# Stores moved to another engine's queue, and sums merged over two hidden units, in the last first layer of a fused attention and feed-forward kernel

## The chip, the cores and the metric

The kernel runs on one core of a Trainium2 chip, in one launch. The metric is device time in microseconds. The engines are TensorE (PE in the profile, its weight loads PEld), VectorE (DVE), ScalarE (ACT), GpSimd (POOL) and SyncE (SP). Any of SP, ACT and POOL can issue a transfer.

## The reference

All data are fp32. An attention block is followed by a feed-forward block on its output:

```python
# q, k, v: (4, 8, 768, 64); centroids: (8, 16, 64)
mask = argmax(q_n @ c_n) [:, None] == argmax(k_n @ c_n) [None, :]
attn = softmax(where(mask, q @ k.T / 8, -1e9)) @ v
x = attn.transpose(0, 2, 1, 3).reshape(4, 768, 512)
xn = (x - mean) / sqrt(var + 1e-6) * g_ln
out = x + maximum(xn @ w_ch1, 0) @ w_ch2      # 512 -> 2048 -> 512
```

## The kernel before, in words

The attention takes the first 318 us of the profiled execution. Then the feed-forward block runs batch by batch, b = 0 to 3. Each batch has a *first layer* (xn @ w_ch1, with the relu) and a *second layer* (with w_ch2, and x added). The first layers are computed at 318 to 390, 466 to 534, 605 to 668 and 737 to 805 us, each followed by its second layer; the program ends at 877.7.

**Fewer products.** Both layers replace a 2x2 block product by seven block products and sums (Strassen's scheme in Winograd's form). In a first layer, `first_layer(b, j, part)` issues one of the parts 1, 2, 6, 5, 7, 4, 3 for unit j; a unit is 128 hidden features of each half of w_ch1's columns, and there are NFH = 8. Each part is four matmuls of 128x384 (L853) into a PSUM bank. `kept` (L877, ACT copies at L879) copies a bank to SBUF, into a tile with the tag "p" (five buffers), when a later part needs it: u2 after part 6, u3 after part 7. `hidden_tile` gives the place of a finished hidden block in SBUF, `add_relu` and `relu` (L890, ACT at L892) complete it. TensorE does the products, DVE the sums.

**Two levels deep.** Second layers of b = 1 to 3 are `deep_layer`: seven ways, each itself seven products of 128x192 (L1149). They need sums of hidden blocks; `outer_sums(c, two)` (L1099) makes them for one unit c with three DVE adds (L1102, L1103, L1105). The finished outputs have features on partitions. `turn` (L1206) turns them by 32x32 transposes on DVE (L1208) into a tile y with the tag "row", of which there are two, and appends eight stores to a list `leaving`, 48 KB each, in runs of 128 B. `leave(n, queues)` issues the first n stores of the list (L1222). It is called from deep_layer and from `unit_end(b, j)`, which runs once for each unit of the next first layer. For b = 1, unit_end calls it also for x_d<-col, 96 KB each, a scratch copy of x for the batches to come.

**The last first layer.** `last_layer(b)`, b = LAST = 3, uses the deeper scheme for three of the seven parts as well. It walks over NPU = 4 pairs of units, g = 0 to 3, with eight slots each. A slot issues one plain part for one unit of the pair, (0,1), (1,1), (0,6), (1,6), (0,7), (1,7), (0,4), (1,4), and after it a few of the inner products A, B and C (`inner_products`, TensorE L1272, sums on DVE at L1281 and L1287, copies on ACT at L1283). B yields `fifth_sum`, the part that both outputs of a unit need. `onto_first` (L1407 to L1412) adds it to u2 and u3 with one DVE add of 128x384 (L1410) per unit and half, in slots 4 and 5 (l = 0) and 6 and 7 (l = 1). Then comes relu for the tiles in `summed`, and outer_sums for the two units of the pair before, one in slot 3 and the other in slot 4.

The orders of PE, DVE, ACT and SP are those of emission, written out by hand. `ring_load` and `last_load` stream weights on SP from scratch in device memory (w<-w_d, and ws<-w_d at L1360). SP also issues all stores of `leave` except in the last deep layer, where they alternate between SP and ACT. POOL issues two stores of y_end (L1504) at the end of the program.

Of the kernel before, what the change touches and what calls it, by code (L numbers as in the profile page):

```python
# [8 lines left out]
F32 = mybir.dt.float32  # L9
# [4 lines left out]
ALU = mybir.AluOpType  # L14
# [9 lines left out]
def kernel(  # L24
# [845 lines left out]
    def hidden_tile(r, f):  # L870

        l, c = divmod(f, NFH)
        h = place((r, l))[:, c]
        hidden[r, l, c] = h
        return h

    def kept(bank, name):  # L877
        t = hid.tile([P, HC], F32, tag="p", name=name, bufs=5)
        nc.scalar.copy(t, bank[:, :HC])  # L879
        return t  # L880

# [13 lines left out]
    def first_layer(b, j, part):  # L895

        _, t1, t2, t4 = normed[b]
        st = sets[b, j]
        s1, s2, s3, s4 = st["s"]
        if part == 1:  # L900
            st["x"] = ps("x_ps")
            product(st["x"], w1_block(0, 0, j), x_block(b, 0, 0), True)
            st["p1"] = kept(st["x"], "p1")
        elif part == 2:
            y = ps("y_ps")
            product(y, w1_block(0, 1, j), x_block(b, 1, 0), True)
            add_relu(0, j, y, st["p1"])
        elif part == 6:
            product(st["x"], s2, t2, False)
            st["u2"] = kept(st["x"], "u2")  # L910
        elif part == 5:
            st["z"] = ps("z_ps")
            product(st["z"], s1, t1, True)
        elif part == 7:
            product(st["x"], s3, x_block(b, 0, 1), False)
            st["u3"] = kept(st["x"], "u3")
            if "z" in st:
                add_relu(1, NFH + j, st["z"], st["u3"])
        elif part == 4:
            product(st["x"], w1_block(1, 1, j), t4, False)  # L920
            nc.scalar.activation(hidden_tile(0, NFH + j), st["x"][:, :HC], AF.Relu)
        elif part == 3:
            product(st["z"], s4, x_block(b, 1, 1), False)
            add_relu(1, j, st["z"], st["u2"])
# [171 lines left out]
        h = h.rearrange("p c (t a r) -> p c t a r", a=2, r=Q)  # L1096
        return [[h[:, l * NQH : (l + 1) * NQH, :, r] for l in range(2)] for r in range(2)]

    def outer_sums(c, two):  # L1099

        a11, a12, a21, a22 = [place((r, l))[:, c] for r in range(2) for l in range(2)]
        nc.vector.tensor_tensor(place("e")[:, c], a21, a22, ALU.add)  # L1102
        nc.vector.tensor_tensor(a21, a11, a21, ALU.subtract)  # L1103
        if two:
            nc.vector.tensor_tensor(place("s")[:, c], place("e")[:, c], a11, ALU.subtract)  # L1105

    def outer_late(o, x, y, n):
# [118 lines left out]


    PAIRED = 2
    LAST = B - 1
    NPU = NFH // 2  # L1230
    w1_d = {n: spill.tile([NPU, P, m], F32, name=f"w1_d{n}") for n, m in ((2, 512), (5, 896), (3, 896), (0, 1024))}
    pairs_of = {}
# [129 lines left out]
    def last_layer(b):  # L1362

        deep_room(b)
        tmp, (_, t1, _, _) = deep[b]["tmp"], normed[b]
        fifth_sum = tmp[:, 2]
        x5 = inner_x(t1, tmp[:, 0])
        x_of = {5: x5}
        t = flat(unit("pi"))
        second = [t[:, i * QC : (i + 1) * QC] for i in range(3)]  # L1370
        third = [last_w["a3"][:, 2 * QC + i * QC : 3 * QC + i * QC] for i in range(2)] + [t[:, 3 * QC :]]
        state = {}

        def first_of(g):

            w = last_w[5]
            return {
                "w": w_operands(*parts_of(w, 3), w[:, 3 * P :]), "x": x_of[5], "onto": None,
                "keep": lambda way: hid.tile([P, HC], F32, tag="p", name="kept", bufs=5)[:, :QC],
                "to": lambda r, h: fifth_sum[:, r * HC + h * QC : r * HC + (h + 1) * QC],  # L1380
            }

        def third_of(g):
            def to(r, h):
                return hidden_tile(1, 2 * g + r)[:, half[h]]

            return {
                "w": w_operands(*parts_of(last_w["a3"], 3), last_w[3]), "x": x_of[3], "onto": to, "to": to,
                "keep": keep_in(third),
            }  # L1390

        def second_of(g):
            (a11, a12), (_, a22) = w1_pair(2 * g)
            return second_pair(b, 2 * g, w_operands(a11, a12, a22, last_w[2]), x_of[2], second)

        makers = {"A": second_of, "B": first_of, "C": third_of}

        def steps(what, g, i):
            if g >= NPU:
                return  # L1400
            if i == 1:
                state[what, g] = makers[what](g)
            inner_products(state[what, g], {1: (1, 2), 2: (6, 5), 3: (7,), 4: (4, 3)}[i])
            if i == 4 and what != "B":
                summed.extend(hidden_tile(int(what == "C"), 2 * g + r) for r in range(2))

        def onto_first(j, l):  # L1407
            h = hidden_tile(1, l * NFH + j)
            first = fifth_sum[:, (j % 2) * HC : (j % 2 + 1) * HC]
            nc.vector.tensor_tensor(h, first, sets[b, j][("u2", "u3")[l]], ALU.add)  # L1410
            if l:
                summed.append(h)  # L1412

        for g in range(NPU):
            j = 2 * g
            for slot, (r, part) in enumerate(
                ((0, 1), (1, 1), (0, 6), (1, 6), (0, 7), (1, 7), (0, 4), (1, 4)), 1
            ):
                if (g, slot) != (0, 1):
                    first_layer(b, j + r, part)  # L1420
                inner = {
                    1: [("C", g - 1, 4), ("B", g, 3)], 2: [("B", g, 4), ("A", g, 1)], 3: [("A", g, 2)],
                    4: [("A", g, 3)], 5: [("A", g, 4)], 6: [("C", g, 1)],
                    7: [("C", g, 2), ("B", g + 1, 1)], 8: [("C", g, 3), ("B", g + 1, 2)],
                }
                if g == 0:
                    inner |= {
                        1: [], 2: [("B", g, 1)], 3: [("B", g, 2), ("A", g, 1)], 4: [("A", g, 2), ("B", g, 3)],
                        5: [("B", g, 4), ("A", g, 3)], 6: [("A", g, 4), ("C", g, 1)],
                    }  # L1430
                elif g == NPU - 1:
                    inner |= {5: [("A", g, 4), ("C", g, 1)], 6: [("C", g, 2)], 7: [("C", g, 3)], 8: [("C", g, 4)]}
                for what in inner[slot]:
                    steps(*what)
                if g == 0:
                    if slot == 2:
                        x_of[2] = inner_x(x_block(b, 1, 0), flat(unit("xi")))
                    if slot == 3:
                        x_sum(b, 3)
                    if slot == 4:  # L1440
                        x_of[3] = inner_x(x_block(b, 1, 1), tmp[:, 1])
                        x_sum(b, 4)
                for r in {4: (0,), 5: (1,)}.get(slot, ()) if g else (0, 1) * (slot == 5):
                    onto_first(j + r, 0)
                if slot in (6, 7):
                    onto_first(j + slot - 6, 1)
                relu(len(summed))
                if slot in (3, 4) and g:
                    outer_sums(j - 5 + slot, True)
                for n, at, ahead in ((0, 7, 1), (5, 3 if g else 5, 1), (3, 2, 0), (2, 6, 1)):  # L1450
                    if slot == at and (ahead or g):
                        last_load(n, g + ahead)
                if slot in (4, 8):
                    unit_end(b, j + slot // 8)
                if slot in (6, 8) and g == NPU - 1:
                    inner_sums(deep[b], ORDER[0], cs=slice(slot - 6, slot - 4))
# [6 lines left out]
    def deep_layer(b, more, st):  # L1463
# [113 lines left out]
        for m, way in STEPS:  # L1577
# [1 line left out]
                ahead_of(m)  # L1579
            deep_product(st, m, way)  # L1580
            ring_load(b)
            leave(2 if more else 4, (nc.sync,) if more else (nc.sync, nc.scalar))
            if way == 1 and b == PAIRED and m == ORDER[0]:
                for cs in (slice(0, NQH - 1), slice(NQH - 1, NQH)):
                    if cs.start:
# [147 lines left out]
    with tc.manual_schedule(engines=order | {mybir.EngineType.SP}):  # L1733
# [4 lines left out]
        def unit_end(b, j):  # L1738
# [4 lines left out]
                else:  # L1743
                    rows_load(b + 1, j + 2)
            if b == 1:
                leave(4)
                if asked and j % 2:
                    columns_load(row)
                if j == 0:
                    outer["ends"] = all_in_range()  # L1750
                if j == 2:
                    outer["flag"] = flag_of(outer.pop("ends"))
                m = (1, 5, 3, 4, 2, 7, 6, None)[j]
                if m in SUMS:
                    split = w2_split(m, outer.pop(("t", SUMS.index(m) + 1)))
                elif m:
                    split = w2_split(m, by_half(w2_block(*{1: (0, 0), 2: (1, 0), 3: (1, 1)}[m])))
                if j in (5, 6):
                    outer_late("s", "e", (0, 0), j - 5)
# [10 lines left out]
                norm_stats(b + 1)  # L1770
            if b + 1 < B and j + 2 == NFH:
                norm_stat_rows(b + 1)
            leave(8 if b >= PAIRED else 4)
            if j == 0 and b + 1 < B:
                rows_load(b + 1, 2)
            if b == 1 and m:
# [274 lines left out]
```

## Time and profile before

| | us |
|---|---|
| median of 3 runs (lowest to highest) | 879.33 (879.27 to 879.78) |
| profiled execution | 879.53 |
| its span in the profile | 877.7 |
| TensorE busy (4744 matmul instructions) | 866.4 |
| DVE busy | 730.3 |
| ACT busy | 409.1 |
| POOL busy | 77.7 |
| DMA read and written | 115.21 MB and 40.07 MB |

The profile shows one execution. The span is the time from its first to its last instruction; 1.8 us of the measured time lie around it. A busy time counts only compute; instructions that issue transfers are shown by queue, SP's as SPq. A row of the page names the line, engine and operation, output and inputs, shape and count, then busy time and mean ns, and the idle time of the engine just before.

### The profile page before, as it was taken

The numbers are of one execution on the slowest core, as the hardware profiler recorded it, in microseconds if no ns is written. First come the engines' busy times: TensorE is split into PE (matmuls) and PEld (weight loads), VectorE is DVE, ScalarE is ACT, GpSimd is POOL, SyncE is SP. The second block draws the span as 40 slices with busy tenths as digits, with TensorE's granted clock in tenths as the row PEclk, the third lists the DMA queues.
The fourth block names the chain that finished last, engine by engine and source line by source line (L and its number), as shares of the span: only waits on it lengthen the run. The fifth ranks groups of instructions, "written<-read, shape, count | busy, mean of one in ns | idle before, by whom it ended". The sixth has DMA issues, their size and how long they took to land.

```text
span 877.7 us, 13639 instructions
## 1 busy us (share of the span) xinstructions
PE 866.4 (99%) x4744; PEld 586.6 (67%) x4744; DVE 730.3 (83%) x1262; ACT 409.1 (47%) x758; POOL 77.7 (9%) x143
## 2 busy tenths in 40 slices
PE   8999999999999999999999999999999999999996
PEld 5444444444444445568886558997667998778996
DVE  6899999999999888958767788887878897768875
ACT  6777788888888834330004542102553111443110
POOL 1011221222222212110000000000000000000000
PEclk9999999999999999999999999999999999999999
DMA  7777799999986428876685988865557875564875
GB/s 161 140 128 129 141 180 188 198 207 198 192 173 189 111 80 221 232 190 237 171 201 175 271 253 297 275 182 159 154 158 251 289 204 143 131 181 134 273 201 105
DMA packets 258493, 164.68 MB, mean 188 GB/s; under 512 B 192992, under 2 KB 211440, under 8 KB 257392
## 3 DMA queue, kind: packets, MB, share of 16 engines
q1 hardware_dynamic: 227392, 144.43, 61.3%
q0 software_dynamic: 7776, 15.03, 8.6%
q10 hardware_dynamic: 23248, 4.25, 2.7%
q8 instruction: 40, 0.66, 0.3%
q14 instruction: 37, 0.30, 0.1%
HBM read 115.21 MB, written 40.07 MB: 177 GB/s over the span
## 4 chain that ended last, share of the span: by engine, by line
PE 95%; DMA 2%; DVE 1%; SPq 1%; ACTq 0%; ACT 0%; issue 0%; DVEq 0%
PE x_ps L853 19%; PE s_ps L401 17%; PE a_ps L413 14%; PE x_ps L1149 12%; PE z_ps L853 7%; PE z_ps L1149 6%; PE x_ps L962 5%; PE y_ps L1149 3%; PE z_ps L962 2%; PE y_ps L853 2%; PE x_ps L1272 2%; PE den_ps L469 1%; PE sim_ps L320 1%; PE y_ps L962 1%; PE z_ps L1272 1%; DMA out_dram<-y_end 1%
## 5 line engine op out<-in xcount | busy, mean ns | idle before, releaser
L401 PE MATMUL s_ps<-t,t 64*128 64x384 f32 x768 | 154.8, 483 | 0.0
L401 PEld LDWEIGHTS s_ps<-t,t 64*128 64x128 f32 x768 | 67.9, 187 | 39.0 <-issue 38.3
L1149 PE MATMUL x_ps<-lower,w 128*128 128x192 f32 x448 | 80.7, 326 | 0.5 <-DVE u L1164 0.5
L1149 PEld LDWEIGHTS x_ps<-lower,w 128*128 128x128 f32 x448 | 74.1, 190 | 1.5 <-DVE u L1164 0.7
L396 ACT ACTIVATE e<-s_ps 128x768 f32<-128x768 f32 x84 | 67.1, 813 | 6.9 <-PE s_ps L401 6.3
L396 ACT ACTIVATE w<-s_ps 128x768 f32<-128x768 f32 x80 | 64.5, 813 | 8.2 <-PE s_ps L401 7.6
L892 ACT ACTIVATE lower<-lower 128x384 f32<-128x384 f32 x88 | 44.1, 521 | 45.0 <-DVE lower L884 30.6
L401 PE MATMUL s_ps<-mask,mask 64*128 64x384 bf16 x384 | 62.8, 323 | 1.0 <-ACT e L396 0.6
L879 ACT COPY u<-x_ps 128x384 f32<-128x384 f32 x64 | 30.7, 479 | 64.3 <-PE x_ps L853 64.0
L413 PE MATMUL a_ps<-e,v_sb 128*64 128x384 f32 x336 | 57.6, 488 | 0.0
L879 ACT COPY p<-x_ps 128x384 f32<-128x384 f32 x32 | 15.3, 478 | 90.5 <-PE x_ps L853 85.3
L413 PE MATMUL a_ps<-w,v_sb 128*64 128x384 f32 x320 | 55.2, 488 | 0.0
L853 PE MATMUL x_ps<-xn,w 128*128 128x384 f32 x128 | 46.6, 487 | 0.0
L853 PE MATMUL x_ps<-xt,ws 128*128 128x384 f32 x128 | 46.6, 487 | 0.0
L853 PE MATMUL x_ps<-xn,ws 128*128 128x384 f32 x128 | 46.6, 487 | 0.0
L853 PE MATMUL x_ps<-xt,w 128*128 128x384 f32 x128 | 46.5, 486 | 0.0
L884 DVE TENSOR_TENSOR lower<-z_ps,u 128x384 f32<-128x384 f32 x40 | 22.2, 554 | 27.8 <-PE z_ps L853 19.9
L413 PEld LDWEIGHTS a_ps<-e,v_sb 128*64 128x64 f32 x336 | 23.5, 137 | 31.8 <-issue 29.3
L1504 POOL DMA_DIRECT2D out_dram<-y_end x2 | 1.2, 597 | 482.0 <-DMA out_dram<-y 482.0
L413 PEld LDWEIGHTS a_ps<-w,v_sb 128*64 128x64 f32 x320 | 22.4, 137 | 30.4 <-issue 27.6
L401 PEld LDWEIGHTS <-mask 64*128 64x128 bf16 x384 | 18.9, 94 | 35.0 <-issue 10.0
L1162 ACT COPY u<-x_ps 128x192 f32<-128x192 f32 x30 | 9.6, 319 | 63.6 <-PE x_ps L1149 59.1
(296 smaller groups left out, 1835.0 us busy)
## 6 DMA issues: line engine op xcount, KB each, us to landing
w<-w_d SPq DMA_DIRECT2D x84, 256.0 KB, 3.3
raw<-in_moe_w_ch_dram SPq DMA_DIRECT2D x32, 512.0 KB, 4.8
w<-w_t SPq DMA_DIRECT2D x36, 256.0 KB, 4.9
w<-tb POOLq DMA_DIRECT2D x32, 256.0 KB, 5.8
w_d<-wt SPq DMA_DIRECT2D x7, 1024.0 KB, 5.0
w<-w_all SPq DMA_DIRECT2D x27, 256.0 KB, 3.1
v_sb<-in_v_dram SPq DMA_DIRECT2D x32, 192.0 KB, 4.7
xr<-x_d SPq DMA_DIRECT2D x24, 256.0 KB, 2.9
```

The source lines that it names most:

```text
L320: nc.tensor.matmul(sim[r : r + Q, :HC], cT[:, pr, :, :].rearrange("p j c -> p (j c)"), prepared[n][side][:, g * HC : (g + 1) * HC], start= ...
L396: nc.scalar.activation(e, s[:, :, :HC], AF.Exp, scale=SCALE)
L401: nc.tensor.matmul(s[:, j, :HC], of_keys[:, keys], of_queries[:, o : o + HC], start=part == first, stop=part != first, skip_group_check=True,)
L413: nc.tensor.matmul(acc[j * D : (j + 1) * D, :HC], loaded[n]["v"][:, j, c, :], e[:, j, :], start=(c == 0), stop=(c == NT - 1),)
L853: nc.tensor.matmul(bank[:, :HC], lhs[:, c, :], rhs[:, c], start=first and c == 0, stop=c == NDH - 1, skip_group_check=True,)
L879: nc.scalar.copy(t, bank[:, :HC])
L884: nc.vector.tensor_tensor(h, bank[:, :HC], other, ALU.add)
L892: nc.scalar.activation(h, h, AF.Relu)
L962: nc.tensor.matmul(bank[:, :MH].rearrange("p (h f) -> p h f", h=2), hidden[lhs + (c,)][:, tt * P : (tt + 1) * P], rhs[:, :, c], start=firs ...
L1149: nc.tensor.matmul(bank, w[:, c, :], a[:, c], start=way in (1, 2, 5) and c == 0, stop=c == NQH - 1, skip_group_check=True,)
L1162: nc.scalar.copy(o, rows_of(of))
L1272: nc.tensor.matmul(bank, p["w"][way], p["x"][way], start=way in (1, 2, 5), stop=True, skip_group_check=True)
```

## The change

Three edits, of which the first concerns batches 1 to 3 and the others the last first layer alone.

1. `leave` gets nc.gpsimd in deep_layer (except in the last one) and at both calls in unit_end. That moves 64 stores out_dram<-y and 12 stores x_d<-col from SP to POOL. The last 24 stores out_dram<-y stay on SP and ACT.
2. In the last first layer, u2 and u3 are copied by ACT straight into the hidden tiles of that unit instead of "p" tiles. `onto_first` adds fifth_sum in place for both units of the pair, in one add of 128x768 for each half; 16 adds become 8. They are issued at the beginning of slot 5 (l = 0; for g = 0 at its end) and of slot 7 (l = 1), ahead of that slot's inner products. The relu of both units then comes in slot 7. 
3. `outer_sums` takes both units of a pair, as 128x768, and one of its three adds is issued in each of slots 2, 3 and 4; 18 adds become 9. For g = 0, `inner_x` of x_of[3] moves from slot 4 to slot 5.

DVE has 17 instructions fewer.

```diff
     def kept(bank, name, t=None):
+        if t is None:
+            t = hid.tile([P, HC], F32, tag="p", name=name, bufs=5)
-        t = hid.tile([P, HC], F32, tag="p", name=name, bufs=5)
         nc.scalar.copy(t, bank[:, :HC])
...
-            st["u2"] = kept(st["x"], "u2")
+            st["u2"] = kept(st["x"], "u2", hidden_tile(1, j) if b == LAST else None)
...
-            st["u3"] = kept(st["x"], "u3")
+            st["u3"] = kept(st["x"], "u3", hidden_tile(1, NFH + j) if b == LAST else None)
...
-    def outer_sums(c, two):
+    def outer_sums(c, two, which=range(3)):
         a11, a12, a21, a22 = [place((r, l))[:, c] for r in range(2) for l in range(2)]
-        nc.vector.tensor_tensor(place("e")[:, c], a21, a22, ALU.add)
-        nc.vector.tensor_tensor(a21, a11, a21, ALU.subtract)
-        if two:
+        if 0 in which:
+            nc.vector.tensor_tensor(place("e")[:, c], a21, a22, ALU.add)
+        if 1 in which:
+            nc.vector.tensor_tensor(a21, a11, a21, ALU.subtract)
+        if two and 2 in which:
             nc.vector.tensor_tensor(place("s")[:, c], place("e")[:, c], a11, ALU.subtract)
...
         def onto_first(j, l):
-            h = hidden_tile(1, l * NFH + j)
-            first = fifth_sum[:, (j % 2) * HC : (j % 2 + 1) * HC]
-            nc.vector.tensor_tensor(h, first, sets[b, j][("u2", "u3")[l]], ALU.add)
+            h = place((1, l))[:, j : j + 2].rearrange("p c t -> p (c t)")
+            nc.vector.tensor_tensor(h, fifth_sum, h, ALU.add)
             if l:
-                summed.append(h)
+                summed.extend(hidden_tile(1, NFH + j + r) for r in range(2))
...
+                if slot == 7 or slot == 5 and g:
+                    onto_first(j, slot // 7)
                 for what in inner[slot]:
                     steps(*what)
                 if g == 0:
...
                     if slot == 4:
+                        x_sum(b, 4)
+                    if slot == 5:
                         x_of[3] = inner_x(x_block(b, 1, 1), tmp[:, 1])
-                        x_sum(b, 4)
-                for r in {4: (0,), 5: (1,)}.get(slot, ()) if g else (0, 1) * (slot == 5):
-                    onto_first(j + r, 0)
-                if slot in (6, 7):
-                    onto_first(j + slot - 6, 1)
+                if slot == 5 and not g:
+                    onto_first(j, 0)
                 relu(len(summed))
-                if slot in (3, 4) and g:
-                    outer_sums(j - 5 + slot, True)
+                if slot in (2, 3, 4) and g:
+                    outer_sums(slice(j - 2, j), True, (slot - 2,))
...
-            leave(2 if more else 4, (nc.sync,) if more else (nc.sync, nc.scalar))
+            leave(2 if more else 4, (nc.gpsimd,) if more else (nc.sync, nc.scalar))
...
             if b == 1:
-                leave(4)
+                leave(4, (nc.gpsimd,))
...
-            leave(8 if b >= PAIRED else 4)
+            leave(8 if b >= PAIRED else 4, (nc.gpsimd,))
```

More of the change, by code (lines that the diff above doesn't have):

```diff
@@ L875, in hidden_tile, with kept @@
         return h
-    def kept(bank, name):
-        t = hid.tile([P, HC], F32, tag="p", name=name, bufs=5)
+    LAST = B - 1
+    def kept(bank, name, t=None):
+        if t is None:
+            t = hid.tile([P, HC], F32, tag="p", name=name, bufs=5)
         nc.scalar.copy(t, bank[:, :HC])
@@ L1228 @@
     PAIRED = 2
-    LAST = B - 1
     NPU = NFH // 2
```

## The prediction

> **What bounds the kernel now.** I began with the page's totals and the shares of the chain that ended last.
>
> ```profile
> PE 866.4 (99%) x4744; PEld 586.6 (67%) x4744; DVE 730.3 (83%) x1262; ACT 409.1 (47%) x758; POOL 77.7 (9%) x143
> PE 95%; DMA 2%; DVE 1%; SPq 1%; ACTq 0%; ACT 0%; issue 0%; DVEq 0%
> ```
>
> TensorE is busy in 866.4 of 877.7 us. A change can help only where TensorE stands idle or a matmul takes longer than its pitch, and hurt only where it makes TensorE wait. So I read the windows by stage next. The first changed instruction comes after 466 us.
>
> ```profile
> 466.00:534.00 68.00, 68.00 (x213) 39.94 (x213) 53.83 (x117) 34.63 (x84) 0.00 (x0) 1.00 0.81 244
> 605.00:668.00 63.00, 63.00 (x225) 40.69 (x224) 50.96 (x146) 33.20 (x81) 0.00 (x0) 1.00 0.55 164
> 737.00:805.00 68.00, 67.83 (x292) 50.37 (x291) 49.05 (x122) 28.27 (x68) 0.00 (x0) 1.00 0.50 139
> 850.00:878.00 28.00, 19.92 (x122) 19.12 (x120) 16.18 (x30) 1.01 (x4) 1.18 (x2) 0.94 0.59 124
> ```
>
> Columns: window, sum, then busy time of PE, PEld, DVE, ACT and POOL, the TensorE clock, DMA share, GB/s. TensorE is full in the first two; the last first layer (737 to 805) lacks 0.17. Only the tail has real idle time, and its stores and sums aren't touched. POOL does nothing in the middle stages, and DVE has 19 of 68 us free in the last first layer.
>
> A wait too short to be idle time shows as a matmul pair with too long a pitch in the chain in order of time (start, length, engine, line, count). A pair of 128x192 normally takes 0.33.
>
> ```profile
> 747.47 0.43 PE x_ps L1272 x2
> 747.90 0.39 PE z_ps L1272 x2
> 748.29 0.33 PE x_ps L1272 x2
> ...
> 757.68 0.41 PE z_ps L1272 x2
> ...
> 785.26 0.56 PE x_ps L1272 x2
> ...
> 797.28 0.37 DVE pi L1281
> 797.67 0.36 DVE lower L1287
> 798.03 0.47 DVE lower L1410
> 798.49 0.48 DVE fifth L1102
> 799.00 0.56 DVE lower L1103
> 799.55 0.47 DVE w L1105
> ...
> 800.87 0.59 PE x_ps L1272 x2
> ```
>
> Excess over 0.33: 0.10+0.06 at 747.5, 0.08 at 757.7, 0.23 at 785.3, 0.26 at 800.9 plus the 0.17 idle before it. Another 0.10 stands at 613.8 (a pair of 0.45, rounded). Together about **1.0 us**: all that the change can recover. Their causes: at 747.5 DVE is behind with its operand sums, after inner_x; at 785.3 a weight load came late, since SP had eight stores to issue ahead of it; at 800.9 L1410 and the three adds of outer_sums stand on DVE ahead of the sums that TensorE needs. The timeline has that SP queue (start, length, queue, line):
>
> ```profile
> 773.08 6.05 SPq L1222 DMA_DIRECT2D out_dram<-y  x8
> 780.35 0.38 SPq L1360 DMA_DIRECT2D ws<-w_d  x1
> ```
>
> Eight stores take SP 6.05 us, 0.76 each; the load that is late is issued at 780.4, behind them.
>
> **What the Trainium skill says.** "DMA: Bandwidth & Descriptors", section "Issuing engines are not separate DMA queues": issuing from another engine saves only sequencer time, for all transfers run on the same 16 engines. The trace agrees so far: SP pays 0.76 per store, and the DMA share has room (0.50 to 0.81). The same page, "Anatomy of one DMA — SWDGE (gpsimd) path", fits 2.0 us + bytes/436e3, an estimate of 2.1 us for 48 KB; the trace's two stores issued by POOL took 3.7, which I use. "SBUF — State Buffer", "Who interferes with whom", says that GpSimd's descriptor generation is locked out while DVE is in a 2-port mode, and infers that tensor_tensor does not block it. POOL's L289 is steady, 0.84 to 1.01 us beside a DVE over 90% busy, and DVE runs tensor_tensor and transposes where the stores will be, so I add nothing. "Perfetto Trace Analysis", "Optimizing Scalar/DVE Operations", puts DVE's overhead on SBUF at about 60 ns per instruction; that is all that merging saves.
>
> **The change, part by part.** *Stores.* 64 stores of 48 KB and 12 of 96 KB move from SP to POOL; the last deep layer's 24 stay on SP and ACT. POOL's cost per store isn't shown for this shape, so I bound it by POOL's own rows and SP's:
>
> ```profile
> L1504 POOL DMA_DIRECT2D out_dram<-y_end x2 | 1.2, 597 | 482.0 <-DMA out_dram<-y 482.0
> L169 POOL DMA_DIRECT2D g_sb<-in_moe_g_ln_dram x1 | 0.9, 925 | 0.0
> out_dram<-y SPq DMA_DIRECT2D x76, 48.0 KB, 2.1
> out_dram<-y_end POOLq DMA_DIRECT2D x2, 24.0 KB, 3.7
> ```
>
> y_end has 192 runs of 128 B and took 597 ns; g_sb, 512 short runs, 925. A 48 KB store has 384 runs: interpolated, 597 + 192/320 × 328 = **0.79 us**; low end 0.6, high end 2.0 (an estimate: about twice g_sb's row, in case the many-dimensional pattern costs more than its runs). Eight take 6.3 us plus 3.7 to land, 10 us (high end 8 × 2.0 + 3.7 = 19.7). What waits is the turn on DVE that reuses the "row" buffer: there are two, and the third turn of a batch takes that of the first:
>
> ```profile
> 754.84 1.84 DVE L1208 STREAM_TRANSPOSE y<-m 128x768 f32<-128x768 f32 x2
> ...
> 772.07 0.98 DVE L1208 STREAM_TRANSPOSE y<-m 128x768 f32<-128x768 f32 x1
> ```
>
> The first buffer's transpose ends near 755.8, its next user starts at 772.1: 16.3 us against 10, **hidden**; in b=2 the gap is 18.2. Behind these stores on POOL stand only the two y_end stores at 867.9, some 85 us later; SP's row loads, which now also wait on POOL's landing, come in earlier stages with the same room. The 12 wide stores (768 runs, by the same slope 1.2 each) come four at a time: 5 us in an otherwise empty queue. POOL pays 64 × 0.79 + 12 × 1.2 = 65 us in all, none on the path. SP loses 76 instructions, about 59 us of queue time (64 × 0.76, and 12 × 0.93, the median of the wide ones), all hidden but the late load: **−0.23** at 785.3. The 0.10 at 613.8 is not of that kind and stays.
>
> *Sums.* Outer_sums for a pair: six adds at a pitch of about 0.5 (0.48+0.56+0.47 per unit, 3.0 in all) become three of 128x768 at 0.95 (L1202's row of that shape), 2.85. onto_first: two of 0.47 become one of 0.95, in place, nothing saved. DVE drops by 17 instructions and about 0.2 us per pair, none on the path by itself. What counts is place: no outer sums in slots where the inner products are due (slot 2, 3, 4 take one each), and g=0's inner_x moves from slot 4 to slot 5. Recovered: 0.16 at 747.5; of the 0.43 at 800.9 some 0.34, as the three adds (1.5 us) no longer stand before L1281, while a 0.95 onto_first still does in slots 5 and 7 (I leave 0.09). The 0.08 at 757.7 may stay: −0.16 − 0.34 = **−0.50**.
>
> *u2 and u3 in the hidden tiles.* ACT's 16 copies have the same shape and only another destination; ACT no longer waits for a "p" buffer (3.4 us of waits in this stage, off the path): 0. The relu of both units now comes in slot 7; ACT is busy 28 of 68 us there, so 0, and if that cover failed the deep layer's first product would be late by one relu, about 0.5.
>
> Sum: −0.23 − 0.50 = **−0.7** against the profiled 879.53 (span 877.7 and 1.8 around it): 878.8. The median is 0.2 below the profiled run, so **878.6**.
>
> **Rivals.** *A: little or nothing is recovered.* The waits only shift to the next late operand; for it speaks that DVE, not SP, ended most of them. 879.3, or a little below. *B: slower, because POOL issues slowly and holds DVE.* Its place is the L1208 turn at 772 and 637. It decides from (16.3−3.7)/8 = 1.57 us per store. At 2.0 the turn is late by 3.4 in the last batch and 1.5 in b=2; about 1 us of slack each leaves some +3: 882. For it speaks that GpSimd has no row for this pattern; against it the 0.6 and 0.93 measured for nearest ones. *C: the 0.95 us add ahead of the inner sums in slots 5 and 7.* TensorE has little slack there in the last pair: +0.3 in each of four pairs is +1.2, so 880.5. Against it, TensorE eats four 1.29 us matmul groups between inner products. *D: the change does not do what it says.* The order of instructions has the stores on POOL and 17 fewer on DVE, so I give this nothing.
>
> **How the numbers follow.** A measurement can tell about 0.2%, 1.76 us. More than that cannot be recovered from 1.0 us of stalls, unless stalls hide in matmuls whose records don't show them; faster gets 0.10. Chances: forecast 0.42, A 0.22, a gain from such unseen waits 0.10, C 0.11, B 0.15, D 0. Forecast, A and most of C (0.08 of it, up to 881.1) lie within 0.2%: same 0.72. B and the rest of C are slower: 0.18. The range runs from 877.7 (all of the 1.0 recovered gives 878.3, and 0.6 of unseen waits) to 880.9, over C but short of B's 882, so that B's 0.15 and some of the gains below stay outside.
>
> **What would show it.** Right: pairs at 0.33 near 747, 785 and 800; POOL's row out_dram<-y x64 near 0.8 us; DVE's wait before L1208 still zero; span about 877.0. Wrong: a wait of L1208 on a DMA, POOL's row over 1.5 us, matmuls that wait for L1281 behind the new 128x768 add, or a span below 876.

## The result, and the profile after

The changed kernel takes **878.49 us** (median of 22 runs, 877.66 to 878.99), the kernel before 879.73 in the 22 runs beside them (878.31 to 881.30). The ratio is 0.9984, with a 95% interval of 0.9977 to 0.9990: a gain of 0.16%, small but clear of 1. In later sets of runs the kernel before had medians of 879.24 to 879.38, so that the difference is 0.8 to 1.2 us. The profiled execution took 878.73 with a span of 877.0, against 879.53 and 877.7.

The totals and the chain shares of the changed kernel, and its window of the last first layer (sum, then PE, PEld, DVE, ACT, POOL busy):

```profile
PE 866.2 (99%) x4744; PEld 587.3 (67%) x4744; DVE 728.7 (83%) x1245; ACT 408.2 (47%) x758; POOL 136.2 (16%) x219
PE 97%; DMA 1%; SPq 1%; DVE 0%; issue 0%; ACT 0%
```

```profile
737.00:805.00 68.00, 68.00 (x298) 51.28 (x297) 48.35 (x107) 28.68 (x69) 18.55 (x24) 1.00 0.48 137
```

POOL works 58.5 us more, and TensorE has no idle time in this window any more (68.00; it lacked 0.17). The places of the long pairs, in the chain in order of time (start, length):

```profile
747.68 0.33 PE x_ps L1276 x2
748.00 0.33 PE z_ps L1276 x2
...
750.27 0.41 PE x_ps L1276 x2
...
757.80 0.41 PE z_ps L1276 x2
...
784.74 0.33 PE x_ps L1276 x2
...
800.59 0.33 PE x_ps L1276 x2
```

A pair takes 0.33 us without a stall. The stalls at 785 (0.23) and at 801 (0.43) are gone. The 0.16 at 747.5 is gone too, but 0.08 has appeared at 750.3; the 0.08 at 758 stays. That makes 0.74.

**Where the time went.** Both traces have 4744 matmuls, so I matched them by order of start. In the changed kernel TensorE is 0.2 us *later* after the first 16 us, long before any edit acts. It is still 0.21 later at matmul 4050 (736 us), so the stores moved before that point changed nothing for it. At matmul 4350 (805 us) it is 0.55 earlier, and stays so to the last matmul. So the change made **−0.76 us, all of it in the last first layer**. I call this the stage's change below: it leaves out what varies from one profile to the next elsewhere (up to 0.4 us each in the first 16 us and near 321 us). As a ratio, 0.76 us is 0.9991, just outside the measured interval. What the rest of the 1.24 us between the two medians is, no run tells.

POOL's rows by form, and the DMA issues with KB and us to landing:

```profile
L1227 POOL DMA_DIRECT2D out_dram<-y x64 | 49.5, 782 | 214.4 <-DVE y L1213 117.8 <-DVE m L1169 85.0 <-DVE wi L1254 6.8
L1227 POOL DMA_DIRECT2D x_d<-col x12 | 8.6, 725 | 121.0 <-DVE col L518 107.1 <-issue 13.9
```

```profile
out_dram<-y POOLq DMA_DIRECT2D x64, 48.0 KB, 3.5
x_d<-col POOLq DMA_DIRECT2D x12, 96.0 KB, 5.6
```

### The profile page after: what moved, and what is told of

Read it like the earlier page. It is cut to its first block, busy times and chain, and to the rows that moved or that the text cites. A ratio compares the mean times of both kernels' runs of the same rounds, so it can differ in the third digit from the quotient of the medians.

```text
span 877.0 us, 13635 instructions
## 1 busy us (share of the span) xinstructions
PE 866.2 (99%) x4744; PEld 587.3 (67%) x4744; DVE 728.7 (83%) x1245; ACT 408.2 (47%) x758; POOL 136.2 (16%) x219
## 4 chain that ended last, share of the span: by engine, by line
PE 97%; DMA 1%; SPq 1%; DVE 0%; issue 0%; ACT 0%
PE x_ps L853 19%; PE s_ps L401 17%; PE a_ps L413 14%; PE x_ps L1154 12%; PE z_ps L853 7%; PE z_ps L1154 6%; PE x_ps L965 5%; PE y_ps L1154 3%; PE x_ps L1276 2%; PE z_ps L965 2%; PE y_ps L853 2%; PE den_ps L469 1%; PE sim_ps L320 1%; PE z_ps L1276 1%; PE y_ps L965 1%; PE y_ps L1276 1%
## 5 line engine op out<-in xcount | busy, mean ns | idle before, releaser
L1227 POOL DMA_DIRECT2D out_dram<-y x64 | 49.5, 782 | 214.4 <-DVE y L1213 117.8
L882 ACT COPY u<-x_ps 128x384 f32<-128x384 f32 x48 | 23.0, 479 | 45.7 <-PE x_ps L853 45.5
L289 POOL DMA_DIRECT2D w<-tb x32 | 28.7, 898 | 98.1 <-DVE tb L286 75.2
```

The source lines that it names most:

```text
L289: nc.gpsimd.dma_start(out=w, in_=fb, accum_op=ALU.add)
L1227: queues[i % len(queues)].dma_start(out=to, in_=y)
```

## The experiments

The ratios and the stage's changes are taken against the kernel before; the line numbers shift a little between kernels. A stage's change comes from one profile, a median from 4 to 22 runs.

| kernel | stage's change, us | median, us | ratio (interval) |
|---|---|---|---|
| changed kernel | −0.76 | 878.49 | 0.9984 (0.9977 to 0.9990) |
| e1: stores alone | −0.58 | 878.51 | 0.9989 (0.9980 to 0.9997) |
| e2: sums alone | −0.76 | 878.54 | 0.9990 (0.9984 to 0.9997) |
| e3: inner_x alone | −0.24 | 879.20 | 0.9999 (0.9990 to 1.0007) |
| e4: outer_sums alone | −0.66 | 878.60 | 0.9992 (0.9984 to 1.0001) |
| e5: before, DVE padded | −0.10 | 879.24 | 0.9997 (0.9989 to 1.0005) |
| e6: onto_first late | −0.77 | 878.28 | 0.9987 (0.9980 to 0.9993) |
| e7: stores on ACT | | 922.42 | 1.0494 (1.0478 to 1.0510) |
| e8: stores thrice on POOL | | 950.78 | 1.0814 (1.0796 to 1.0832) |
| e9: before, stores in two | | 894.98 | 1.0181 (1.0166 to 1.0197) |
| e10: POOL's stores in two | −0.76 | 878.49 | 0.9992 (0.9983 to 1.0000) |
| e11: POOL's stores in four | | 902.51 | 1.0261 (1.0245 to 1.0277) |
| e12: the last stores on POOL too | −0.76 | 879.21 | 1.0000 (0.9991 to 1.0008) |

### The parts alone

**e1, the stores.** Edit: the three calls of `leave` with nc.gpsimd, nothing else.

> The kernel before with the moved stores alone (64 out_dram<-y and 12 x_d<-col on POOL). Theory (late weight load behind SP's stores): the matmul pair at 785 us falls from 0.56 to 0.33, the other long pairs (747, 758, 801) stay, TensorE reaches the deep layer of the last batch 0.2 us earlier, time about -0.2 us. Rival 1 (the stores matter more in unprofiled runs than in the one profile, which would explain why the medians differ by 1.2 us where the two profiles differ by 0.75): time -0.7 us or more. Rival 2 (the load is late for another reason): the pair at 785 stays at 0.56, time 0.0.

Measured: −0.58 in the stage, almost three times what the theory gave.

```profile
785.01 0.33 PE x_ps L1272 x2
...
800.86 0.42 PE x_ps L1272 x2
```

The pair at 785 is at 0.33, and the pairs at 747.5 and 758 stay, as the theory had it; but the stall at 801 also fell from 0.43 to 0.09, with the adds on DVE in their old places. Rival 1's "−0.7 or more" is inside the interval of the ratio, but the profile says that 0.34 of it comes from a place where no store is near.

**e2, the sums.** Edit: the changed kernel with

```diff
-            leave(2 if more else 4, (nc.gpsimd,) if more else (nc.sync, nc.scalar))
+            leave(2 if more else 4, (nc.sync,) if more else (nc.sync, nc.scalar))
...
-                leave(4, (nc.gpsimd,))
+                leave(4)
...
-            leave(8 if b >= PAIRED else 4, (nc.gpsimd,))
+            leave(8 if b >= PAIRED else 4)
```

> The changed kernel with its stores back on SP: the sums, in-place u2 and u3 and inner_x edits alone. Theory: pairs at 747 and 801 fall to 0.33, the one at 785 stays at about 0.56, TensorE reaches the last deep layer 0.5 us earlier, time -0.5 us. Rival 1 (the gain is the stores'): time within 0.1 of before. Rival 2 (the two parts need each other, since the sums set the room for the late load): the pair at 785 grows or vanishes, and e1 and e2 do not add up to the change's 0.77 us of TensorE time.

Measured: −0.76, the whole change, with all stores still on SP.

```profile
784.16 0.33 PE x_ps L1276 x2
...
800.02 0.33 PE x_ps L1276 x2
```

So e1 and e2 do not add up (−1.34 against −0.76): rival 2's second half holds. Both take away the stall at 801, all of it or most, and the one at 785 isn't there in every execution. The medians of e1, e2 and the changed kernel lie within 0.05 us of each other: with either part in place, the other adds nothing that they show.

**e3 and e4.**

```diff
                     if slot == 4:
-                        x_of[3] = inner_x(x_block(b, 1, 1), tmp[:, 1])
                         x_sum(b, 4)
+                    if slot == 5:
+                        x_of[3] = inner_x(x_block(b, 1, 1), tmp[:, 1])
```

> The kernel before with only inner_x of x_of[3] moved from slot 4 to slot 5 for g = 0. Theory: the two pairs at 747.5 and 747.9 fall from 0.43 and 0.39 to 0.33 (-0.16), nothing else moves; time -0.1 to -0.2. Rival (the sums at 747 are late for another reason, the inner products before it): both pairs stay and time is unchanged.

Measured: the two pairs at 747 are at 0.33, and the next one is long in their place, in the chain of e3:

```profile
747.07 0.33 PE x_ps L1272 x2
747.39 0.33 PE z_ps L1272 x2
...
749.66 0.48 PE x_ps L1272 x2
```

0.15 of the 0.16 has moved by one slot. The stage's −0.24 is the stall at 785, again absent with the stores on SP. Neither statement was quite right: inner_x was the cause at 747, and its new place makes the next sum late.

e4 has the edit of outer_sums alone: a pair at a time, in slots 2, 3 and 4.

> The kernel before with only outer_sums changed: both units of a pair in one add of 128x768, one add in each of slots 2, 3 and 4. Theory (the three adds stand ahead of the inner sums in slot 4 of the last pair): the idle time and the long pair at 801 go, or most of their 0.43, time -0.3 to -0.4. Rival (L1410 ahead of the sums is the cause, so it needs onto_first moved): 0.2 or more of it stays, time -0.2 or less; a 0.95 add ahead of sums elsewhere may also cost some 0.1.

Measured: −0.66, of which 0.43 is the whole stall at 801 and the rest the absent one at 785.

```profile
800.50 0.33 PE x_ps L1274 x2
```

L1410 stayed where it was, so it was not the cause. That it was the three adds alone does not follow from this run, as the next section shows.

### Why the stores alone freed the stall at 801

The chain from 797 us to the pair at 801 begins on DVE with the inner sum that writes the tile pi (L1281). DVE's timeline (start, length, idle before), before:

```profile
796.25 0.55 DVE L1105 TENSOR_TENSOR w<-fifth,lower 128x384 f32<-128x384 f32 x1
797.28 0.36 DVE L1281 TENSOR_TENSOR pi<-x_ps,p 128x192 f32<-128x192 f32 x1 [0.48 <-ACT u L879]
```

and in e1:

```profile
796.41 0.55 DVE L1105 TENSOR_TENSOR w<-fifth,lower 128x384 f32<-128x384 f32 x1
797.09 0.36 DVE L1281 TENSOR_TENSOR pi<-x_ps,p 128x192 f32<-128x192 f32 x1
```

The records are the same; before, pi starts 0.48 after L1105 ended, in e1 0.13. The trace has a record for the wait just ahead of pi: before, pi starts 0.40 us after that wait has passed, in e1 0.04. The releaser named (the copy of u) isn't one, for in e1 pi starts while that copy still runs (796.70 to 797.18). The long chain at 797 to 801 thus contained a delay of 0.35 that no wait explains. e3 has it too:

```profile
796.63 0.36 DVE L1281 TENSOR_TENSOR pi<-x_ps,p 128x192 f32<-128x192 f32 x1 [0.48 <-ACT u L879]
```

I counted DVE's records from the start, waits included, in groups of 128. The delayed pi is number 63 of its group in both kernels; in e1 it is number 76. At places 61 to 64 of other groups stand similar gaps of 0.39 to 0.42 us where DVE has just passed a wait, and none where it works without a pause. The traces hold a control that nobody had planned: another pi, near 657 us, is number 59 before and in e2, e3 and e4, and starts 0.04 us after its wait. In the changed kernel and in e1 it has four more records ahead of it, is number 63, and starts 0.40 us after its wait (TensorE loses nothing there). The trace also shows a transfer of 8 KB in the queue of kind "instruction" 0.7 to 0.9 us after the delayed pi at 797 (798.22 before, 797.32 in e3); in e1 there is none of that size between 791 and 809. I took this for a boundary of instruction fetch, and the waits on POOL's landings for what shifted it. The test:

```diff
+    pads = const.tile([P, 16], F32, name="pads")
...
                 leave(4)
+                for i in range(13 * (j == 3)):
+                    nc.vector.memset(pads[:, i : i + 1], 0.0)
```

> The kernel before (stores on SP, sums as before) with 13 more instructions on DVE, memsets of one unused column each, near 500 us where DVE has room. Why: in the profile before and in e3 the sum pi (L1281) at 797 starts 0.40 us after the instruction ahead of it although all it waits for is done; in e1, where DVE's program has 13 instructions more ahead of it (the waits on POOL's landings), it starts after 0.04. In all six profiles a gap of 0.39 to 0.42 stands at one fixed place of DVE's program, every 128 instructions, where DVE is not running behind its queue. Theory (a boundary of instruction fetch; e1's gain at 801 is its shift, not the stores): the gap before pi goes, the stall at 801 falls from 0.43 to about 0.1 as in e1, TensorE -0.34 there; time -0.3, to -0.6 if the stall at 785 is absent too. Rival (POOL taking SP's stores is what freed pi): the gap and the stall at 801 stay, time 0.0.

Measured, in the chain and in DVE's timeline of e5:

```profile
782.30 0.59 PE x_ps L1273 x2
...
785.16 0.53 PE x_ps L1273 x2
...
800.57 0.41 PE x_ps L1273 x2
```

```profile
796.12 0.55 DVE L1106 TENSOR_TENSOR w<-fifth,lower 128x384 f32<-128x384 f32 x1
796.80 0.36 DVE L1282 TENSOR_TENSOR pi<-x_ps,p 128x192 f32<-128x192 f32 x1
```

The gap before pi is 0.13 again and the stall at 801 is down to 0.08, with the stores on SP. So the gain of e1 at 801 is the shift of the program; POOL has a part in it only through the 13 waits that its stores put into DVE's program. (e9 below agrees: its pi is number 65, starts 0.04 us after its wait, and the stall is 0.35 smaller, with the adds in their old places and the stores on SP.) What the boundary is inside the chip, the runs don't show; that it is tied to a place in DVE's program they do.

This also limits what e2 and e4 say. They have fewer instructions on DVE, so that pi is number 52 and 58 there, and in the changed kernel 65: the delay is gone from all of them. Without the delay the three adds cost 0.08 to 0.09 (e1, e5); what moving them does while the delay stands, no run tested. An estimate from e4's timeline: the last sum that the pair needs (a, L1283) ends 0.41 us before the weight load that waits for it, just over the 0.35. In the changed kernel the weight load already waits 0.2 us for that sum, at no cost to TensorE yet, so part of the stall would be back there. Part of the changed kernel's gain is then the luck of where pi falls.

The stage gained only 0.10 in e5, because weight loads came late twice, 0.26 and 0.20, at 782 and 785: the waits there are on a<-w_d and ws<-w_d. Its median is 0.14 below that of the kernel before, with an interval that holds 0 and 0.34 alike, so the shift's gain is shown by the profiles and not by the medians. Of the five profiles with the stores on SP (before, e2 to e5) two have a late weight load: SP's third group of eight stores took 6.05 us before and 6.46 in e5, and 5.78 to 5.93 in the three without. Of the five with the stores on POOL (changed kernel, e1, e6, e10, e12) none has. So few profiles do not prove it; the next run asks directly.

### Is it SP's queue?

Edit, to the kernel before (e10 and e11 apply it to the changed kernel, e11 with 4):

```diff
-            queues[i % len(queues)].dma_start(out=to, in_=y)
+            m = 2 if len(queues) == 1 and len(to.shape) == 4 and to.shape[1] == NT else 1
+            for c in range(0, Q, Q // m):
+                queues[i % len(queues)].dma_start(out=to[c : c + Q // m], in_=y[c : c + Q // m])
```

> The kernel before (stores on SP) with each of the 64 stores out_dram<-y that the change would move cut into two of 24 KB over its partitions, so that SP issues 16 per turn ahead of the weight loads. Theory (the loads behind SP's stores are late by what SP spends on stores): SP's group at 773 grows from 6.0 to some 10 us, the loads a<-w_d and ws<-w_d behind it come 4 us later, and the stalls at 782 to 785 (0.23 in the profile before, 0.46 in e5, none in e2 to e4) grow to 3 to 4 us; the groups at 756 and 763 have less close behind them. Time +3 to +5 us. Rival (those stalls are the chance of a slow landing and not SP's queue): stalls stay below 0.5, time within 0.5 us.

Measured: +15.7 us; in the profile TensorE is 14.5 late at the end, 11.3 of it from matmul 4050 to 4350. SP's timeline and the waits of TensorE in the last first layer (total, times, longest):

```profile
759.01 10.30 SPq L1224 DMA_DIRECT2D out_dram<-y  x16
769.41 0.54 SPq L1359 DMA_DIRECT2D a<-w_d  x1
...
771.00 10.31 SPq L1224 DMA_DIRECT2D out_dram<-y  x16
...
782.51 10.80 SPq L1224 DMA_DIRECT2D out_dram<-y  x16
793.42 0.54 SPq L1359 DMA_DIRECT2D a<-w_d  x1
```

```profile
PEld x_ps L1274 <- DMA a<-w_d: 7.7, 2, 4.0
PEld x_ps L853 <- DMA ws<-w_d: 2.1, 1, 2.1
```

Three groups of over 10 us come every 12 us, so SP never catches up, and TensorE waits some 4 us for each of two loads a<-w_d and 2 for ws<-w_d: more than the theory's 3 to 5 us, since I had counted only the group at 773. The same cut on POOL costs nothing (e10), so it is SP's queue and not the number of transfers. The mechanism is the one that the prediction gave for the 0.23, and its edge lies close: with 6 us in the third group the stall is 0 to 0.5, with over 10 in each group it is 11 in this stage.

### How slow may POOL be?

**e10** (cut in two) lies below the point that the prediction gave for rival B, **e11** (cut in four) above it.

> The changed kernel with the same cut into two: 128 stores of 24 KB on POOL, 192 runs each as y_end's, 0.60 us, so 1.2 us for each 48 KB. This is below the 1.57 us from which rival B decides (16 x 0.6 = 9.6, and 2.4 to 3.7 to land, 12 to 13 us against 16.3). Theory: L1213 does not wait on a transfer, time within 0.5 us of the changed kernel. Other (any added POOL work or descriptor writing slows DVE): DVE's transposes or sums get longer, +1 us or more.

> The same cut into four: 256 stores of 12 KB, some 0.55 us each, 2.2 us per 48 KB, above rival B's point: 32 x 0.55 = 17.6 and 2.4 to 3.7 to land, 20 to 21 us against 16.3 in the last batch and 18.2 in b=2. Theory (B's mechanism): L1213 waits on DMA some 4 us at 772 and 2 us near 638, TensorE about 1 us less in each: +3 to +5 us. Other (the turn has more room than thought): L1213 waits, time within 1 us of the changed kernel.

POOL's rows of e10 and of e11:

```profile
L1229 POOL DMA_DIRECT2D out_dram<-y x128 | 80.4, 637 | 190.2 <-DVE y L1213 109.1 <-DVE m L1169 80.2 <-DMA out_dram<-y 0.8
```

```profile
L1229 POOL DMA_DIRECT2D out_dram<-y x256 | 172.6, 680 | 150.2 <-DVE y L1213 86.8 <-DVE m L1169 58.6 <-issue 3.1
```

e10 costs 2 × 0.637 = 1.27 us per 48 KB and changes nothing: TensorE's offset to the changed kernel is the same within 0.01 us from 531 us to the end, and L1213 waits for no transfer. POOL's extra work doesn't slow DVE either: DVE's transposes of 128x768 take 968 ns in e10, 968 in the changed kernel and 967 before. e11 costs 4 × 0.680 = 2.7 us and +23 us. In its waits from 610 to 700 us and in those of SP:

```profile
DVE qs L1128 <- DMA w_d<-qs: 9.1, 1, 9.1
PE z_ps L1154 <- DMA w<-w_t: 7.6, 1, 7.6
DVE y L1213 <- DMA out_dram<-y: 5.6, 1, 5.6
```

```profile
SPq L609 <- DMA out_dram<-y: 14.3, 1, 14.3
```

The turn waits 5.6 us here and 7.8 in the last batch, as rival B had it, with 32 × 0.68 = 21.8 us of issuing. The larger part in this stretch is a second way that rival B did not have: SP's load of stat_row (L609) waits for the landings of POOL's stores, 14.3 us, and the scratch stores w_d<-qs and the weight loads w<-w_t queue up behind it. The prediction had named that wait and costed it at nothing, which holds at 0.78 and at 1.27 us per 48 KB, and no longer at 2.7.

**e8** was meant as a milder form of the same: `for _ in range(3)` around the store on POOL.

> The changed kernel with each store that POOL issues issued three times in a row (the same data to the same place), so that a store costs POOL about 2.35 us in place of 0.78. Theory (rival B of the prediction, its mechanism and its point of 1.57 us): eight take 18.8 us and some 4 to land, against 16.3 us until the turn (L1213) at 772 needs the buffer and 18.2 in b=2: that turn waits about 6.5 and 4.6 us on POOL's transfers; less the slack behind the turn, +4 to +10 us. Other theory (nothing near the end of those buffers is on the path): L1213 waits, but the time stays within 1 us.

Measured: +71.4 us, far off, because the dose was not the one intended. In this program POOL waits, before it repeats a store to the same place, until the one before has landed. POOL's own waits:

```profile
POOL out_dram L1228 <- DMA out_dram<-y: 65.7, 45, 3.8
```

The x_d<-col stores were tripled too. DVE's turn then waits for these transfers (23.9 us in four waits), but the price per store isn't the one that was to be tested; e10 and e11 replace it.

**e7, another queue:** nc.scalar in place of nc.gpsimd in the changed kernel.

> The changed kernel with the moved stores on ACT's queue, not POOL's. Theory (what makes the move free is that POOL has nothing else to do): eight stores at 0.65 to 0.76 are 5 to 6 us in which ACT copies no PSUM bank and does no relu; six such groups in b=2 and b=3 and three of x_d, each costing TensorE up to some 2 to 4 us: +10 to +25 us. Rival (ACT is only 40 to 50% busy there, so any queue does): time within 1 us of the changed kernel.

```profile
ACT p L882 <- DMA out_dram<-y: 70.7, 7, 17.6
PEld x_ps L853 <- ACT p L882: 23.0, 6, 7.3
```

+43 us. ACT's copies of PSUM banks stand behind stores that first wait for DVE's turn and then take 5 us a group; TensorE waits for the banks. The theory's direction holds, its size was half or less: I had counted the issuing, not the waiting for the turn that a queue in order takes over with each store.

### The long add, and the last stores

**e6:** `onto_first` after the inner products of slots 5 and 7. The inner sums of C then start from hidden tiles to which the fifth product isn't added yet, so part of the hidden values lacks it; only the time is read.

> The changed kernel with the two merged adds of onto_first (128x768, 0.95 us) issued after the inner products of slots 5 and 7, not ahead of them. Theory (the 0.95 us ahead of the inner sums lies under TensorE's plain products): TensorE's time from 737 to 805 is within 0.1 of the changed kernel, time 0.0 beside it. Rival C of the prediction (a long add ahead of inner sums costs up to 0.3 per pair): the pairs at 750 and 758, 0.41 each in the changed kernel, fall to 0.33 and time is 0.1 to 0.2 lower. Third: relu comes later and the last pair's hidden blocks are late: slower by 0.3 to 0.5 at 801 to 805.

Measured: −0.77 in the stage against −0.76, the pairs at 750 and 758 still 0.41, and 0.08 lost again in the deep layer. The 0.95 us ahead of the inner sums costs nothing: rival C is out.

**e12:** the last deep layer's 24 stores on POOL as well.

> The changed kernel with the last deep layer's 24 stores on POOL too, in place of SP and ACT in turn. Theory (those on the way to the end are rightly left on two queues): the last groups of four take POOL 3.1 us in place of 1.3 on SP and on ACT, the y_end store behind them on POOL is late by about 0.5, and the program ends 0.3 to 1 us later. Rival (ACT's issues ahead of its last copies, 0.6 each in the chain of the profile before, are what the end waits for): the end comes 0.3 to 1 us earlier, and this is a better version.

The chain that ended last, and POOL's timeline at the end:

```profile
871.38 1.04 POOLq L2050
872.42 0.55 POOL out_dram L1508
```

```profile
861.81 10.06 POOL L1227 DMA_DIRECT2D out_dram<-y  x13
871.86 1.12 POOL L1508 DMA_DIRECT2D out_dram<-y_end  x2
```

The y_end stores stand behind 10 us of others, start at 871.9 in place of 867.4, and POOL now ends the chain. The median is 0.7 above that of the changed kernel, which is the theory's direction and size. The profile alone wouldn't show it: the program ends 7.1 us after the last matmul began, against 6.95 in the changed kernel, but 7.16 in the kernel before, whose last stores stand on two queues. No complete kernel run here beats the changed one; e6, 0.2 below it, leaves out a part of the hidden values.

## Why the prediction was right

The forecast was 878.6, −0.7 by its sum; measured were 878.49 and −0.76 in the trace. The sum came out better than its terms deserve: of the three terms −0.23, −0.16 and −0.34 the profile gave −0.23, −0.08 and −0.43, so that one miss of 0.08 and one of 0.09 cancel. That is luck.

- **Stores, POOL's price.** Estimated 0.79 us and 3.7 to land; measured 0.782 and 3.5. The value is right and the interpolation over runs is not: 384 runs took 0.782, but 192 took 0.637 (e10), 96 took 0.680 (e11) and the 96 KB store with 768 runs 0.725, where the slope gave 1.2. POOL's price hardly depends on the runs here. Hidden, as worked out; the point of 1.57 us lies between e10 (1.27) and e11 (2.7), which does not prove it to a tenth.
- **Stores, −0.23 at 785.** The cause fits (e9, with twice the stores), but the term is not a constant. It was a stall of this one profile; e2, e3 and e4 have none with the same queue, e5 has 0.46. What the move buys is freedom from a stall that comes in some executions; in the medians of e2 and the changed kernel (878.54 and 878.49) it doesn't show.
- **Sums, −0.16 at 747.5.** Mis-sized: the stall moved by one slot, to 0.08 at 750.3 in the changed kernel (0.15 in e3 alone).
- **Sums, −0.34 at 801.** Measured −0.43, the whole. The step failed in its reading: I put it all on the adds ahead of L1281, but 0.34 to 0.35 of it goes, with the adds in their old places, when DVE's program shifts by 13 instructions and the delay before pi vanishes (e1, e5). That this is the 0.34 of the forecast is a coincidence. The adds and that delay had to meet. Taking away the delay alone leaves 0.08 to 0.09; the kernels that move the adds lost the delay as well, so that the adds alone were never tested. A 0.48 of idle time before pi stood in the trace of before, and I did not ask what ended it.
- **u2 and u3 in place, relu later: 0.** Holds: the 0.95 add is as priced (952 and 949 ns, DVE's groups below), and TensorE has no wait on it at 805.

```profile
L1413 DVE TENSOR_TENSOR lower<-qs,lower 128x768 f32<-128x768 f32 x8 | 7.6, 952 | 0.1
L1106 DVE TENSOR_TENSOR fifth<-lower 128x768 f32<-128x768 f32 x3 | 2.8, 949 | 0.0
```

- **Rivals.** A (little recovered) and C (the long add costs) are out. B has its mechanism and is far from deciding at 0.78. The Trainium skill, "DMA: Bandwidth & Descriptors", section "Issuing engines are not separate DMA queues", says that another issuing engine saves only the sequencer's time, usually small beside the transfer. The runs agree in that the stores land no faster on POOL (3.5 against 2.1 us). The time on the queue is not small here: SP takes 0.65 to 0.8 us per store, and twice the stores cost 16 us (e9).

## What to carry to other kernels

A queue that works in order holds up whatever stands behind its waits: move stores to the queue that has nothing else, and price not only the issuing but the wait for the data that the queue takes over, and who waits for those landings later. A stall read in one profile is one draw: ask how much slack the landing has, and look at a second profile before it enters a sum as a constant. Where an instruction starts late though everything it waits for is done, suspect its place in the program. An edit that adds or removes instructions also shifts all that follow, and can take the credit for what the shift did: test the shift alone with unused instructions, and the edit with the shift undone.

## What the runs showed of the hardware that was not expected

DVE starts an instruction 0.35 us later than usual at a fixed place in groups of 128 records (waits included), where it has just passed a wait; 13 unused instructions move it. For the sum pi it can be counted: in the fourteen profiles it is number 63 right behind a wait eight times, and starts 0.40 us after it each time; at other numbers, 89 times, 0.04 to 0.15 us after it. POOL's price for a store is nearly flat, 0.64 to 0.78 us for 96 to 768 runs of 128 B (rows of the changed kernel, e10 and e11).
